# A third buffer for the weights of the first FFN layer, loads issued by two engines, and a new issue order, in a fused attention and FFN kernel

## The chip, the cores and the metric

The kernel runs on one core of one Trainium2 chip. The metric is the device time of one execution in microseconds (us), the median of several runs. One execution of each kernel was also recorded by the hardware profiler.

## The reference

One transformer block on x of 2048 rows and 576 columns, all in bf16. Attention has 32 heads of 18 and works in four segments of 512 rows: inside a segment it is causal softmax attention, and what came in earlier segments is read from a small memory M with its norm z. The FFN goes from 576 to 4608 and back. Cut to what matters:

```python
# in attention, on layernorm(x); for each segment s of 512 rows
logits = einsum('bhqd,bhkd->bhqk', qs, ks) * scale + mask
a_dot = einsum('bhqk,bhkd->bhqd', softmax(logits), vs)
pq = phi(qs)                                   # t + 1 if t > 0, else exp(t)
a_mem = einsum('bhld,bhde->bhle', pq, M) / (einsum('bhld,bhd->bhl', pq, z) + 1e-6)
o = g * a_mem + (1 - g) * a_dot                # g = sigmoid(beta)
M, z = M + phi(ks)^T @ vs, z + sum(phi(ks))
# then
h  = x + o @ wo
h2 = h + (gelu(layernorm(h) @ w1 + b1) @ w2 + b2)
```

## The kernel before

One function computes all of it, in eight chunks of 256 rows (two tiles of 128). For each chunk there are these streams of work:

- P: layernorm of a tile of x, its transpose xT, the products with wq, wk and wv (L612, and L613 for the last 65 of the contraction's rows), and their eviction from PSUM to qk_pad and v_aug (L706 to L711). The first chunk is transposed by TensorE (L657 for x, L755 for qk_pad) and moved by L692 and L693; later ones by DMA transposes, all through the helper at L367, which SP issues. xT, QT, KT, o_col and xn2T come from there.
- A: scores (L841, TensorE in a tiling of 32 rows), exp of 2048 columns at a time by ScalarE (L847), the causal mask by GpSimd or VectorE (L852, L854), and weighted values (L873, in a tiling of 32 columns). M is built at L799 and read at L910.
- B: the product with wo (also through L612), the residual, the second layernorm, and its transpose xn2T. h goes out to DRAM as hd and comes back later as hc.
- F1: the first FFN layer. F is cut into 9 groups of 512 columns. A group has four "tails" (the last 64 rows of the contraction, L1185, in a tiling of 64 rows) and 16 main matmuls (L1198); VectorE or ScalarE adds b1 on the way out of PSUM (L1208, L1206), and ScalarE applies gelu (L1220). A part of chunk 0 goes another way (L1158, L1160, with xz holding the tail rows).
- F2: the second layer (L1254), its eviction with the residual (L1258) and the output DMAs (L1265, L1267).

Short matmuls of pq with itself ("fillers", L1326) keep TensorE going while nothing else is ready at the start. They need pq, which VectorE clears (L568).

w2 stays in SBUF. w1 doesn't: each group is loaded again for each chunk, 512 KB for the mains (L1105) and two pieces of 32 KB for the tails (L1108). Two buffers, w1g0 and w1g1, take the loads in turn; the first loads also go into three pieces of the second hidden buffer hT1 while that is unused, and from load 45 on three pieces of the buffer of wq, wk and wv are used as well, since these are no longer needed.

All DMAs are issued by SP: the inputs (x at L531, weights at L534 and L535, beta at L576), w1 and w2 (L1112), the transposes, and the way out and back of h (hd, hc).

The order of the work comes from three things. A planner written into the kernel generates the operations of the streams, each with an estimated duration and with the tiles that it reads and writes. `ORDER` is a long table of operation numbers, the order in which they are issued; a negative number takes the other engine of an operation that two engines can do (`either`). `PLACE` gives the PSUM bank of each use. The engines run their queues in this order, so a waiting instruction holds up what stands behind it on its engine. What of the order concerns one engine is shown in the section on the change.

Of the kernel before, what the change touches and what calls it, by code (L numbers as in the profile page):

```python
# [16 lines left out]
def kernel(  # L17
# [41 lines left out]
    def sbuf(name, shape, dt=BF16):  # L59
# [294 lines left out]
    def transfer(o, kb, first, rd, wr, receipt=0.0):  # L354
# [3 lines left out]
        note(d, rd, wr)  # L358
        mark(d, rd, wr)
        return d  # L360

    def dma(kb, issue, rd=(), wr=(), slack=0.0):
        return transfer(op("SP", 0.5, issue, rd, wr, slack), kb, 1.6, rd, wr, {288: 0.1, 144: 0.7, 576: 0.8, 72: 0.6, 864: 1.4}.get(kb, 1.0))

    def dma_t(blocks, dst, src, rd, wr, slack=0.0):

        o = op("SP", 1.25, lambda: nc.sync.dma_start_transpose(out=dst, in_=src), rd, wr, slack)  # L367
        return transfer(o, blocks * 45 + 70, 1.4, rd, wr, 0.2)

    def begin(o, eng=None):  # L370
# [1015 lines left out]
```

## Time and profile before

| | us |
|---|---|
| median of 3 runs (lowest, highest) | 459.45 (458.41, 460.61) |
| the profiled execution | 458.34 |
| its span in the trace | 456.6 |
| TensorE busy | 448.5 |
| ScalarE busy | 315.3 |
| VectorE busy | 286.9 |
| GpSimd busy | 147.4 |
| DMA bytes moved | 83.39 MB |

The span runs from the first to the last recorded instruction; the execution's time has 1.74 us around it. In the profile's rows PE is TensorE's matmuls, PEld its loads of weights, DVE VectorE, ACT ScalarE, POOL GpSimd and SP SyncE; SPq marks the issuing of a DMA on SP's queue. A row of the timeline has its start, its duration, the engine, the line, the operation, output and inputs, the count of equal rows that it stands for, and in brackets the idle time before it with what ended that. A row of the list of waits has the waiting engine, tile and line, what it waited for, and then the total, the count and the longest wait.

### The profile page before, as it was taken

How to read it: one execution, taken by the hardware profiler on the slowest of the kernel's cores; microseconds unless marked ns; L12 is line 12 of the kernel's file. 1: busy time of each engine (PE TensorE's matmuls, PEld its weight loads, DVE VectorE, ACT ScalarE, POOL GpSimd, SP SyncE). 2: the span in 40 equal slices, each digit the busy share in tenths (PEclk: the TensorE clock that was granted, in tenths of full speed). 3: DMA queues.
4: the chain of work that ended last, by engine and by line, in shares of the span. 5: the costliest groups of instructions: out<-in, count | busy, mean ns of one | idle time of the engine just before them, and what ended most of it. 6: DMA issues, size and time to landing. Idle time of an engine off the chain costs nothing.

```text
span 456.6 us, 14417 instructions
## 1 busy us (share of the span) xinstructions
PE 448.5 (98%) x6074; PEld 333.2 (73%) x6074; DVE 286.9 (63%) x761; ACT 315.3 (69%) x316; POOL 147.4 (32%) x202
## 2 busy tenths in 40 slices
PE   7999999999999999999999999999999999999997
PEld 5776776666777777776567777667788888888874
DVE  6998888887786767876765686678672532211101
ACT  5999889976887965797786876978932354366230
POOL 4776423564373033436512333233210020000000
PEclk9999999999999999999999999999999999999999
DMA  7989998969798987787796679987778767575001
GB/s 227 329 252 264 193 184 201 182 176 178 166 251 156 232 202 178 195 177 135 204 176 165 180 194 165 201 201 156 192 193 213 196 194 191 161 208 157 27 14 39
DMA packets 137491, 83.39 MB, mean 183 GB/s; under 512 B 72786, under 2 KB 135634, under 8 KB 137426
## 3 DMA queue, kind: packets, MB, share of 16 engines
q1 hardware_dynamic: 137426, 82.47, 76.5%
q8 instruction: 47, 0.77, 0.7%
q14 instruction: 18, 0.15, 0.1%
HBM read 59.43 MB, written 6.49 MB: 144 GB/s over the span
## 4 chain that ended last, share of the span: by engine, by line
PE 89%; DMA 5%; SPq 3%; ACT 1%; DVE 1%; issue 1%; ACTq 0%
PE bank L1254 21%; PE bank L1198 17%; PE bank L612 13%; PE late L1254 6%; PE late L1198 6%; PE st L841 5%; PE ox L873 4%; PE bank L613 3%; PE bank L1185 3%; PE bank L1158 2%; PE ox L1254 1%; PE ox L1198 1%; SPq L367 1%; DMA hT<-in_B_w_dram 1%; DMA w1g<-in_B_w_dram 1%; DMA beta_row<-in_A_beta_dram 1%
## 5 line engine op out<-in xcount | busy, mean ns | idle before, releaser
L847 ACT ACTIVATE pt<-st 128x2048 bf16<-128x2048 f32 x80 | 150.1, 1877 | 41.9 <-PE st L841 21.2
L1254 PEld LDWEIGHTS <-hT 128*128 128x128 bf16 x1152 | 109.4, 98 | 29.6 <-issue 0.8
L1254 PE MATMUL bank<-w_sb,hT 128*128 128x288 bf16 x864 | 126.3, 286 | 0.0
L1198 PE MATMUL bank<-xn2T,w1g 128*128 128x256 bf16 x656 | 85.3, 273 | 0.0
L852 POOL TENSOR_SCALAR_AFFINE_SELECT pt<-pt 128x512 bf16<-128x512 bf16 x81 | 52.4, 658 | 95.2 <-ACT pt L847 88.8
L1198 PEld LDWEIGHTS <-w1g 128*128 128x128 bf16 x768 | 71.4, 98 | 16.2 <-issue 6.1
L1208 DVE TENSOR_TENSOR hT<-bank,b1T 128x512 bf16<-128x512 f32 x70 | 47.3, 685 | 41.5 <-PE bank L1198 41.1
L1220 ACT ACTIVATE hT<-hT 128x1536 bf16<-128x1536 bf16 (+3 forms) x24 | 65.7, 2768 | 0.2
L612 PE MATMUL bank<-wqkv,xT 128*128 128x432 bf16 (+1 forms) x268 | 57.1, 336 | 0.9 <-DMA xT<-xn 0.8
L612 PEld LDWEIGHTS <-xT 128*128 128x128 bf16 x400 | 36.9, 97 | 19.8 <-DMA xT<-xn 0.9
L1206 ACT ACTIVATE hT<-late,b1T 128x256 bf16<-128x256 f32 x32 | 13.3, 477 | 38.7 <-PE late L1198 22.3
L1258 DVE TENSOR_TENSOR ot<-bank,hc 128x288 bf16<-128x288 f32 x24 | 11.0, 456 | 43.0 <-PE bank L1254 38.0
L1206 ACT ACTIVATE hT<-bank,b1T 128x256 bf16<-128x256 f32 x56 | 23.5, 473 | 20.1 <-PE bank L1198 20.1
L1254 PE MATMUL late<-w_sb,hT 128*128 128x288 bf16 (+1 forms) x216 | 33.9, 296 | 0.0
L841 PE MATMUL st<-QT,KT 32*128 32x128 bf16 x1280 | 32.4, 217 | 0.5 <-issue 0.5
L841 PEld LDWEIGHTS <-KT 32*128 32x128 bf16 x1280 | 18.7, 92 | 15.2 <-issue 11.9
L1198 PEld LDWEIGHTS <-wqkv 128*128 128x128 bf16 x272 | 26.0, 98 | 4.6 <-issue 0.8
L854 DVE TENSOR_TENSOR pt<-pt,causal 128x512 bf16<-128x512 bf16 x47 | 22.4, 479 | 8.3 <-ACT pt L847 8.1
L646 POOL TENSOR_TENSOR rstd_b<-rstd_b,mhalf 128x1 f32<-128x1 f32 x16 | 9.3, 582 | 56.2 <-DVE rstd_b L636 53.8
L873 PE MATMUL ox<-pt,v_aug 128*32 128x128 bf16 x1184 | 26.3, 221 | 0.0
L873 PEld LDWEIGHTS <-v_aug 128*32 128x32 bf16 x1184 | 17.2, 96 | 10.6 <-issue 8.2
L613 PE MATMUL bank<-wqkv,xT 65*128 65x432 bf16 (+1 forms) x67 | 22.6, 338 | 0.0
(156 smaller groups left out, 642.0 us busy)
## 6 DMA issues: line engine op xcount, KB each, us to landing
w1g<-in_B_w_dram SPq DMA_DIRECT2D x50, 512.0 KB, 4.1
wqkv<-in_B_w_dram SPq DMA_DIRECT2D x17, 512.0 KB, 3.9
w_sb<-in_B_w_dram SPq DMA_DIRECT2D x6, 864.0 KB, 7.7
hd<-h_t SPq DMA_DIRECT2D x14, 288.0 KB, 4.2
hc<-hd SPq DMA_DIRECT2D x28, 144.0 KB, 2.9
w1g<-in_B_w_dram SPq DMA_DIRECT2D x100, 32.0 KB, 3.2
x_b<-in_A_x_dram SPq DMA_DIRECT2D x18, 144.0 KB, 3.0
hT<-in_B_w_dram SPq DMA_DIRECT2D x5, 512.0 KB, 6.0
```

Of the source, the lines that this page charges most:

```text
L612: nc.tensor.matmul(out=out_ap, lhsT=lhsT_of(slice(0, P), k), rhs=rhs_of(slice(0, P), k), start=(k == 0), stop=False)
L613: nc.tensor.matmul(out=out_ap, lhsT=lhsT_of(slice(0, KTAIL), 4), rhs=rhs_of(slice(0, KTAIL), 4), start=False, stop=True)
L841: nc.tensor.matmul(out=st4[:, i, n * P:(n + 1) * P], lhsT=KTs[(c - c % 2 + kt // 2) % 3][rows, g, (kt % 2) * P:(kt % 2 + 1) * P], rhs=QTs[ ...
L847: op("ACT", 1.88, lambda: nc.scalar.activation(out=pt[:], in_=st4[:], func=ACT.Exp, scale=scale), sk, [("pt", slot, n) for n in range(4)], ...
L852: either(("POOL", 0.64, lambda part=part: nc.gpsimd.affine_select(out=part, in_=part, pattern=[[0, 4], [1, P]], compare_op=ALU.is_ge, fill ...
L854: ("DVE", 0.42, lambda part=part: nc.vector.tensor_tensor(out=part, in0=part, in1=causal[:].unsqueeze(1).to_broadcast([P, 4, P]), op=ALU.m ...
L873: nc.tensor.matmul(out=ox[32 * i:32 * i + 32, g % 4 * P:(g % 4 + 1) * P], lhsT=v_flat[(2 * s0 + kt) % 6][:, h * E:h * E + 32], rhs=pts[slo ...
L1198: nc.tensor.matmul(out=bank(b)[:, a * Q:(a + 1) * Q], lhsT=w1_main(wt)[:, k, (2 * (h % 2) + a) * P:(2 * (h % 2) + a + 1) * P], rhs=xn2T[c ...
L1206: nc.scalar.activation(out=hT[:, f + a, :], in_=bank(b)[:, a * Q:(a + 1) * Q], func=ACT.Identity, bias=b1T[:, f + a:f + a + 1])
L1208: either(("DVE", 0.69, lambda hT=hT, f=f, b=b: nc.vector.tensor_tensor(out=hT[:, f:f + 2, :], in0=bank(b)[:].rearrange("p (a w) -> p a w", ...
L1220: op("ACT", (f1 - f0) * Q * 0.00083 + 0.18, lambda hT=hT, f0=f0, f1=f1: nc.scalar.activation(out=hT[:, f0:f1, :], in_=hT[:, f0:f1, :], fun ...
L1254: nc.tensor.matmul(out=acc, lhsT=hT[:, q, tl * P:(tl + 1) * P], rhs=w2_sb[:, q, hs], start=(q == 0), stop=(q == NF - 1))
```

## The change

- w1 gets three buffers (w1g0 to w1g2). The loads ahead of use become groups 0 to 5, later ones follow a period of three, and of six from load 45 on. A group's matmuls may be planned only once its load has been.
- Room for that: xn2T has three buffers instead of four, so that the transpose of chunk c waits for the first layer of chunk c - 3. beta_row, ones and b1_rows move into the bytes of t1, and xz into those of t2, both of which are written from later chunks on.
- `dma_two` lets a DMA be issued by SP or by ScalarE. It is used for the first four loads of x, the weights of attention, beta, b1, b2, and all of w1.
- The first two tiles of x come in two halves of 64 rows each, and wq, wk and wv in two halves of 288 columns, each with a key of its own, so that a product needs only its half.
- After attention the five PSUM banks of scores and weighted values become banks 3 to 7 of `PLACE`.
- `ORDER` and `PLACE` were searched anew, with longer issues of SP in the planner's picture of it.

All lines move down: L1105 becomes L1121, L1108 L1124, L612 L628, L657 L673, L755 L771, L847 L863, L1254 L1271, L1326 L1343, L367 L373.

The core of the diff (the table's lines left out):

```diff
+    def dma_two(kb, issue, rd=(), wr=(), slack=0.0):
+        o = either(("SP", 0.5, lambda: issue(nc.sync)), ("ACT", 0.55, lambda: issue(nc.scalar)), rd, wr, slack)
+        return transfer(o, kb, 1.6, rd, wr, {288: 0.1, 144: 0.7, 576: 0.8, 72: 0.6, 864: 1.4}.get(kb, 1.0))
...
-    w1_bufs = [sbuf(f"w1g{j}", [W1]) for j in range(2)]
+    w1_bufs = [sbuf(f"w1g{j}", [W1]) for j in range(3)]
...
+    NX = 3
-    xn2T = [sbuf(f"xn2T{j}", [KT, Q]) for j in range(4)]
+    xn2T = [sbuf(f"xn2T{j}", [KT, Q]) for j in range(NX)]
...
+    early = t1[:].rearrange("p h e -> p (h e)").bitcast(BF16)
+    ones, beta_row, b1_rows = early[:, 0:P], early[:, P:P + H], early[:, 2 * P:3 * P]
+    xz = t2[:].rearrange("p h e -> p (h e)").bitcast(BF16)[:, 0:2 * Q].rearrange("p (h q) -> p h q", h=2)
...
     for tl in range(2):
-        load_x(tl, x_p[tl], ("x_p", tl))
+        for h in range(2):
+            dma_two(72, lambda e, tl=tl, h=h: e.dma_start(out=x_p[tl][64 * h:64 * h + 64, :], in_=x[tl * P + 64 * h:tl * P + 64 * h + 64, :]),
+                    (), [("x_p", tl, h)])
     for j, W in enumerate((A_wq, A_wk, A_wv)):
-        weights(wqkv, slice(j * D, (j + 1) * D), W, f"wqkv{j}")
+        for h in range(2):
+            to = slice(j * D + h * HALF, j * D + (h + 1) * HALF)
+            dma_two(290, lambda e, to=to, h=h, W=W: e.dma_start(
+                out=wqkv[:, 0:4, to], in_=W[0:512, h * HALF:(h + 1) * HALF].rearrange("(k p) n -> p k n", p=P)), (), [f"wqkv{j}{h}"])
...
-                yield need(lambda: c < 4 or c - 4 in done_F1, idle=False)
-                dma_t(KT, xn2T_part, xn2[tl][:], [("xn2", tl)], [("xn2T", c % 4, tl)], SLACK["t_h"])
+                yield need(lambda: c < NX or c - NX in done_F1, idle=False)
+                dma_t(KT, xn2T_part, xn2[tl][:], [("xn2", tl)], [("xn2T", c % NX, tl)], SLACK["t_h"])
...
-        dma(512, lambda: nc.sync.dma_start(out=w1_main(wt), in_=B_w1[0:512, fcols].rearrange("(k p) f -> p k f", p=P)), (), [k], SLACK["w1"])
+        dma_two(512, lambda e: e.dma_start(out=w1_main(wt), in_=B_w1[0:512, fcols].rearrange("(k p) f -> p k f", p=P)), (), [k], SLACK["w1"])
```

What the new tables do to an engine's queue is seen in its rows (line, operation, output and inputs, shape). VectorE at the very start, before: the memsets of padding come ahead of that of pq, on which the fillers wait.

```order
L539 MEMSET ones 1x128
L539 MEMSET xn_1_86 128x32
L539 MEMSET qk_pad_96 128x64x7
L539 MEMSET v_aug_101 128x32
L568 MEMSET pq 128x256
L539 MEMSET maskcol 128x1
```

And in the changed kernel:

```order
L583 MEMSET pq 128x256
L548 MEMSET maskcol 128x1
L548 MEMSET v_aug_96 128x32
L548 MEMSET v_aug_98 128x32
L548 MEMSET v_aug_99 128x32
L548 MEMSET qk_pad_92 128x64x7
```

The memset of pq has moved to the front. On TensorE, 22 fillers now stand ahead of the first transposes instead of 13, and 4 instead of 10 behind them; then the product of the first tile with the first half of wq comes ahead of the second tile's transposes, which stood ahead of all products before.

SP around the first transpose of chunk 4's xn2T (that is xn2T_92 here), before: w1g_67 and w1g_68 are the two buffers of w1, 128x4x512 a group's mains and 64x256 one of its two tails.

```order
L367 DMA_TRANSPOSE KT_108<-qk_pad_97 128x8x128
L1105 DMA w1g_68<-in_B_w_dram 128x4x512
L367 DMA_TRANSPOSE xn2T_92<-xn_0_87 128x5x128
L1108 DMA w1g_68<-in_B_w_dram 64x256
L367 DMA_TRANSPOSE xT_91<-o_nat_114 128x5x128
L367 DMA_TRANSPOSE KT_108<-qk_pad_96 128x8x128
L1105 DMA w1g_67<-in_B_w_dram 128x4x512
L1108 DMA w1g_67<-in_B_w_dram 64x256 x2
```

The same place in the changed kernel, where that tile is xn2T_90 and the buffers are w1g_65 to w1g_67:

```order
L373 DMA_TRANSPOSE xT_87<-o_nat_110 128x5x128
L1256 DMA hc<-hd 128x288
L1124 DMA w1g_67<-in_B_w_dram 64x256
L1074 DMA hd<-h_t_120 128x576
L373 DMA_TRANSPOSE xn2T_90<-xn_0_84 128x5x128
L1124 DMA w1g_66<-in_B_w_dram 64x256 x2
L1121 DMA w1g_66<-in_B_w_dram 128x4x512
L1124 DMA w1g_67<-in_B_w_dram 64x256 x2
L1121 DMA w1g_67<-in_B_w_dram 128x4x512
```

Three transposes stood between the loads of two groups, and now the loads of two groups follow on one transpose.

ScalarE between the first gelu (L1220) and the next evictions of FFN values, before: exps (L847, of the scores st into pt) with the small work of the other streams.

```order
L1220 ACTIVATE hT_128<-hT_128 128x3584
L847 ACT_TABLE_LOAD
L847 ACTIVATE pt_111<-st_155 128x2048
L710 CAST qk_pad_97<-bank_149 128x24x18
L710 CAST v_aug_101<-bank_150 128x8x18
L847 ACTIVATE pt_112<-st_155 128x2048
```

The same place in the changed kernel:

```order
L1237 ACTIVATE hT_124<-hT_124 128x3584
L863 ACT_TABLE_LOAD
L863 ACTIVATE pt_107<-st_151 128x2048
L726 CAST qk_pad_92<-bank_147 128x16x18
L1121 DMA w1g_67<-in_B_w_dram 128x4x512
L726 CAST v_aug_96<-bank_147 128x8x18
L1124 DMA w1g_66<-in_B_w_dram 64x256
L863 ACTIVATE pt_108<-st_151 128x2048
L912 ACTIVATE ek<-QT_102 128x512
L1124 DMA w1g_67<-in_B_w_dram 64x256
L863 ACTIVATE pt_107<-st_151 128x2048
```

Loads of w1 now stand between the exps, in ScalarE's own queue. At the other end of the program, the last product on TensorE before was 20 matmuls of 144 columns behind 20 of 432; now the 144 columns come earlier, and the last are 24 matmuls of 432 columns.

More of the change, by code (lines that the diff above doesn't have):

```diff
@@ L453, in bank @@
         return banks["bank", place[k.serial]] if isinstance(k, Bank) else banks[k]
-    beta_row = sbuf("beta_row", [H])
-    ones = sbuf("ones", [P])
     wqkv = sbuf("wqkv", [KT, 3 * D])
@@ L512, with dynamic_swap @@
     late = []
-    def swap():
+    def dynamic_swap():
         st_pool.__exit__(None, None, None)
@@ L517, in swap @@
         for i in range(4):
-            banks["st", i] = pool.tile([P, 512], F32, name=f"late{i}")
+            banks["bank", 3 + i] = pool.tile([P, 512], F32, name=f"late{i}")
+        banks["bank", 7] = ox
     bank_slots.free.append("ox")
@@ L575, in constants @@
         memset("DVE", 0.06, mhalf[:], -0.5, "mhalf")
-        dma(9, lambda: nc.sync.dma_start(out=beta_row[0:1, :], in_=A_beta.rearrange("(o h) -> o h", o=1)), (), ["beta"])
+        dma_two(9, lambda e: e.dma_start(out=beta_row[0:1, :], in_=A_beta.rearrange("(o h) -> o h", o=1)), (), ["beta"])
         memset("POOL", 0.12, causal[:], BIG, "causal")
@@ L582, in constants @@
         for tl in range(2):
-            layernorm(f"p{tl}", x_p[tl][:], ("x_p", tl), xn1[tl], ("xn1", tl), False, SLACK["ln0"] + 3 * tl, late_scale=True)
+            layernorm(f"p{tl}", x_p[tl][:], ("x_p", tl), xn1[tl], ("xn1", tl), False, SLACK["ln0"] + 3 * tl, late_scale=True,
+                      also=[("x_p", tl, h) for h in range(2)])
         for j in range(2, 6):
@@ L621, in half @@
         def half(c):
-            op("DVE", 0.455, lambda: nc.vector.bn_stats(out=stats[:, c, :], in_=src[:, c * HALF:(c + 1) * HALF]), [skey], ["st" + who],
+            op("DVE", 0.455, lambda: nc.vector.bn_stats(out=stats[:, c, :], in_=src[:, c * HALF:(c + 1) * HALF]), [skey, *also], ["st" + who],
                slack=slack)
@@ L650, in layernorm @@
            slack=slack + SLACK["pow"], port=False)
-        op("DVE", 0.8 if f32 else 0.43, apply, ["st" + who, skey] + ([] if late_scale else ["rs" + who]), [dkey], slack=slack + fast,
+        op("DVE", 0.8 if f32 else 0.43, apply, ["st" + who, skey, *also] + ([] if late_scale else ["rs" + who]), [dkey], slack=slack + fast,
            port=True).two = f32
@@ L1002, in stream_A @@
                             done_A.add(c)
-        bank_slots.free.append("ox")
-        st = [("st", i) for i in range(4)]
-        op("POOL", 0.0, swap, (), st, slack=-1000, port=False)
-        bank_slots.free += st
+        more = [("bank", 3 + i) for i in range(5)]
+        op("POOL", 0.0, dynamic_swap, (), [("st", i) for i in range(4)] + ["ox"] + more, slack=-1000, port=False)
+        bank_slots.free += more
         late.append(True)
@@ L1134, in stream_F1 @@
         for c in range(NCH):
[L1135 removed]
+            xk = [("xn2T", c % NX, 0), ("xn2T", c % NX, 1)]
             hT = hTs[c % 2]
@@ L1176, in stream_F1 @@
                 wk = [key for _, k in w1s for key in (k, (*k, 0), (*k, 1))]
-                yield need(lambda: c in done_B and (c < 2 or c - 2 in done_F2), bank_slots, xk + wk, mode=64, n=2 * len(some))
+                yield need(lambda: c in done_B and (c < 2 or c - 2 in done_F2) and some[-1] < w1_next[0], bank_slots, xk + wk, mode=64,
+                           n=2 * len(some))
                 bs = [bank_slots.take() for _ in range(2 * len(some))]
```

62 lines of the change are left out of this document (32 added, 30 removed), and 231 rows, old and new, of the table ORDER.

## The prediction

> **What bounds the kernel now.** I read the page's busy times first, then TensorE's list of waits, then the timeline at both ends and the chain of waits behind the two longest stops.
>
> ```profile
> span 456.6 us, 14417 instructions
> PE 448.5 (98%) x6074; PEld 333.2 (73%) x6074; DVE 286.9 (63%) x761; ACT 315.3 (69%) x316; POOL 147.4 (32%) x202
> ```
>
> TensorE (PE) is busy for 448.5 of 456.6 us, so the end is set by TensorE's own work plus 8.1 us in which it stands still. The profiled execution took 458.34 us, 1.74 us around its span, and lies 1.11 us below the median of 459.45 us. I make the sum against 458.34 and move the result up by 1.11 at the end. TensorE's waits, each with its total, its count and its longest:
>
> ```profile
> PE ox L1326 <- DVE maskcol L539: 2.0, 1, 2.0
> PE bank L1185 <- DMA w1g<-in_B_w_dram: 0.9, 1, 0.9
> PE bank L612 <- DMA xT<-xn: 0.8, 1, 0.8
> PE st L841 <- issue: 0.5, 1, 0.5
> PE bank L1198 <- DMA hT<-in_B_w_dram: 0.4, 1, 0.4
> PE bank L612 <- DMA xT<-o_nat: 0.3, 1, 0.3
> PE bank L550 <- DMA beta_row<-in_A_beta_dram: 0.2, 1, 0.2
> PE bank L1160 <- issue: 0.2, 1, 0.2
> ```
>
> Of the 8.1 us, 2.0 stand ahead of the first matmul, 3.3 are the seven stops below that row, and the other 2.8 lie in the end behind the last matmul. Transfers are late for only 2.4 us (0.9 + 0.8 + 0.4 + 0.3) after the start. That is the most that loads which come earlier can give there. The change leaves TensorE's products as they are (6079 matmuls instead of 6074, and the five are fillers), so a gain has to come out of the 8.1 us.
>
> **The two long stops** have the same history. The chain of waits around 211 and 234 us, and the mean landing time of a group's load from the page:
>
> ```profile
> 211.93 4.12 DMA xT<-xn
> 233.33 1.21 SPq L367
> 234.59 4.79 DMA w1g<-in_B_w_dram
> w1g<-in_B_w_dram SPq DMA_DIRECT2D x50, 512.0 KB, 4.1
> ```
>
> SP issues everything, and each DMA transpose (L367) holds its queue for over 1.2 us. The w1g tail that TensorE wanted at 239.43 was issued at 234.59 behind such rows, and then took 4.79 us. With two buffers a group's load can start only when the group two before it has been read; with three it is asked for one group earlier. I added up TensorE's durations from the trace between the last read of a buffer's old content and the first read of its new one, in both issued orders: the median is 12.2 us before and 16.9 after, and mains with less than 8 us fall from 17 of 67 to 2 of 66. Against 4.1 us to land, the two stops on w1 (0.9 and 0.4, the latter in the spare buffers) should go nearly to nothing; I leave 0.1. The xT stops (0.8 + 0.3) hang on transposes, and these stay on SP. SP has 348 issues instead of 416, so its pile-ups are shorter; I leave 0.7 of 1.1. **Waits: 2.4 becomes 0.8, so -1.6 us**; bounds -2.4 (none is left) and +1.0 (a new stop as long as the longest of these rows).
>
> **The start.** Rows of the timeline (start, duration):
>
> ```profile
> 1.68 0.27 DVE L568 MEMSET pq<- 128x256 uint32 x1
> 2.01 0.82 PE L1326 MATMUL ox<-pq 128*128 128x256 bf16 x3 [2.01 <-DVE maskcol L539]
> 3.05 1.91 PE L1326 MATMUL bank<-pq 128*128 128x256 bf16 x8
> 4.75 0.74 PE L657 MATMUL ox<-ident,xn 128*128 128x128 bf16 x5
> 5.29 1.50 PE L1326 MATMUL bank<-pq 128*128 128x256 bf16 x10
> 7.10 0.45 PE L657 MATMUL bank<-ident,xn 128*128 128x128 bf16 x5
> 7.50 0.65 PE L612 MATMUL bank<-wqkv,xT 128*128 128x288 bf16 x4
> 7.59 0.49 DVE L693 COPY xT<-bank 128x640 bf16<-128x640 bf16 x1 [1.54 <-PE bank L657]
> 9.00 0.50 ACT L706 ACTIVATE qk_pad<-bank,rstd_p 128x288 bf16<-128x288 f32 x1 [1.60 <-PE bank L613]
> ```
>
> The fillers (L1326) need pq. VectorE clears it at 1.68 behind other memsets; in the new order it does this first, so TensorE can start near 0.88 + 0.27, about 1.2. Eight fillers start from 3.05 to 4.75, 0.2125 us each; the ten from 5.29 take 1.50 in all, so the last ones run at about half of that (0.11, an estimate), from some 3.8 us after TensorE's first row. The new order has 22 fillers ahead of the first transposes: 18 of 0.2125 bring TensorE to 5.0, 4 of 0.11 to 5.45. Then come five transposes (0.45), the copy of xT (0.49, under four more fillers), and the first product at about 6.35 instead of 7.50: 1.15 earlier, without the wait for beta. About 0.5 is given back: the eight transposes of qk_pad (L755) now come right behind the second half of wq's product and five transposes of 0.45, and both halves have to be evicted before (0.50 each, the row at 9.00). **Start: -0.65**; bounds -1.15 and +0.3 (both evictions uncovered, and wq's second half late).
>
> Whether the weights are there is seen in the windows of one us (columns: five engines, granted clock, busy share of the DMA engines, GB/s):
>
> ```profile
> 3.00:4.00 1.00, 1.00 (x7) 0.70 (x5) 0.87 (x3) 1.00 (x4) 0.00 (x0) 1.00 0.72 152
> 4.00:5.00 1.00, 1.00 (x8) 0.70 (x7) 0.96 (x4) 0.52 (x2) 0.00 (x0) 1.00 0.95 311
> ```
>
> Ahead of the first product must land: x (288 KB), two tails of 72 KB and one half of wq (288 KB), 720 KB, that is 2.3 us at 311 GB/s from about 2 us on. So the halves, not the second issuer, free this path. The share of 0.72 in 3 to 4 us is the only gap in which a quicker issue could put bytes. Here a rule speaks against part of the change. The Trainium skill, page "DMA: Bandwidth & Descriptors", section "Issuing engines are not separate DMA queues", says that DMAs begun by several engines run on the same 16 DMA engines, and that only the issuing time is saved. The row of 0.72 agrees that no more than 0.28 us of DMA time is open there; by the rule alone the start would gain about 0.3 and the time would be 458.8 us.
>
> **Array modes.** Counted over both programs, TensorE goes from one tiling of the array to another 288 times instead of 280. A piece of 12 matmuls that ends in such a change, and one of 8 that ends without:
>
> ```profile
> 301.29 1.64 PE L1254 MATMUL bank<-w_sb,hT 128*128 128x288 bf16 x12
> 302.86 0.41 PE L873 MATMUL ox<-pt,v_aug 128*32 128x128 bf16 x16
> ...
> 105.95 1.14 PE L1254 MATMUL bank<-w_sb,hT 128*128 128x288 bf16 x8
> ...
> 106.93 0.30 PE L910 MATMUL bank<-MZ_blk,pq 128*128 128x76 bf16 x4
> ```
>
> From start to start 8 take 0.98, 0.1225 each; 12 would take 1.47 and take 1.57, so a change is 0.10 us. **Eight more: +0.8**; bounds +0.4 and +0.9.
>
> **The end.**
>
> ```profile
> 452.83 0.61 DVE L1258 TENSOR_TENSOR ot<-late,h_t 128x432 bf16<-128x432 f32 x1 [3.32 <-PE late L1254]
> 453.47 1.13 SPq L1265 DMA_DIRECT2D out_dram<-ot  x2
> 453.93 0.31 DVE L1258 TENSOR_TENSOR ot<-ox,h_t 128x144 bf16<-128x144 f32 x1 [0.49 <-PE ox L1254]
> ```
>
> The last product is now 144 columns wide (eviction 0.31); in the new order it is 432 wide (0.61), +0.30. Of the two output DMAs of the second row, issued at 453.47 and 454.27, the wide one landed after 1.67 us and the narrow one after 1.49, +0.18. **End: +0.5**; bounds 0 (if the wide DMA is split over free engines just as fast) and +0.6.
>
> **What ScalarE (ACT) issues.** The new program gives it 73 DMAs: seven at the start, 33 between the exps, and the rest where only the second layer's work is left. It also loads activation tables 14 times instead of 12. The window from 40 to 130 us, the exps, and SP's issues of loads:
>
> ```profile
> 40.00:130.00 90.00, 88.98 (x1486) 63.43 (x1484) 75.27 (x199) 74.76 (x71) 42.24 (x54) 1.00 0.92 191
> L847 ACT ACTIVATE pt<-st 128x2048 bf16<-128x2048 f32 x80 | 150.1, 1877 | 41.9 <-PE st L841 21.2
> ...
> 234.59 0.59 SPq L1108 DMA_DIRECT2D w1g<-in_B_w_dram  x1
> ...
> 17.73 2.24 SPq L1105 DMA_DIRECT2D hT<-in_B_w_dram  x1
> ```
>
> No row shows an issue by ScalarE. Its nearest are SP's for the same loads: 0.59 without a crowd, 2.24 in one. I take 0.59, since the load that I compare with is the same and ScalarE issues them singly between exps. In the part of the program that answers to 40 to 130 us stand 13 of them: 13 x 0.59 = 7.7 us, inside ScalarE's idle 90.0 - 74.76 = 15.2. So the cover is that idle time: **0 us on TensorE**. If the cover is gone, all of it is paid. A wait that ScalarE now takes on itself is new: a main that has to wait until TensorE has read the buffer holds up the next exp behind it, and TensorE's weighted values (L873) wait for that exp. SP shows how long such waits can be:
>
> ```profile
> SPq L1105 <- PE late L1198: 13.8, 8, 3.9
> SPq L1105 <- PE bank L1198: 6.3, 5, 3.9
> ```
>
> Bounds: 0 (below nothing is excluded, as a busier ScalarE speeds nothing up) and 13 x 2.24 - 15.2 = +13.9.
>
> **At no cost**: xn2T with three buffers (a transpose then waits for the first layer of three chunks before, work that lies some tens of us back; its cost, if that fails, is one transpose's 1.21 us on SP). beta, ones, b1 and xz lie in t1 and t2, which are written only in later chunks. The swap of PSUM banks falls after attention. The x halves add two issues at the start.
>
> **Sum**: -1.6 - 0.65 + 0.8 + 0.5 + 0 = -0.95; 458.34 becomes 457.4, and on the median **458.5 us**. Its own range is 456.8 to 460.5 us.
>
> **The rivals.**
> - A, all transfers are on time: waits -2.4, start -1.15, the two "issue" stops of 0.7 moved away by the new order, modes +0.8, end +0.5: -2.95, **456.5 us**. For it speaks the median lead of 16.9 us; against it, that the xT stops lie on transposes.
> - B, slower: ScalarE's issues hold up the exps between 40 and 130 us. The point from which it decides is 15.2 / 13 = 1.17 us for each. At 1.5 us (13 x 1.5 = 19.5, 4.3 over the cover) the sum is -0.95 + 4.3 = +3.35, **462.8 us**. For it: 2.24 in a crowd, and SP's waits of up to 3.9 on the buffers. Against it: 0.59, and a third buffer that is free earlier.
> - C, the change does not do what it says: the stops come from SP's transposes, and a third buffer leaves them. The waits of 2.4 stay, so start -0.65, modes +0.8 and end +0.5 are left, +0.65: **460.1 us**. For it: both long stops have an L367 row in their chain; against it, the leads.
> - D, the rule on issuers above, as a mechanism here: the start gains 0.3 and the rest is as forecast, **458.8 us**.
>
> **Chances.** About 0.5% (2.3 us) is what a measurement of this kernel can tell from no change: 457.15 to 461.75. The forecast has 0.30, C 0.12, D 0.08: within the bound 0.50. A and times below it 0.31; B 0.19. The range leaves out about 0.2: below 455.3 (A with no price for modes and end either, -2.95 - 1.3 = -4.25, 455.2) 0.08, above 463.0 (B beyond 1.5 us each) 0.10.
>
> **What would show it.** Right: the first filler near 1.2 and the first product near 6.35 us; no stop of TensorE on w1g or hT over 0.3 us; ScalarE's issues near 0.6; the last eviction 0.61. Wrong: a list of TensorE's waits with pt or st behind ScalarE at the head (B), xT still at 1.1 (C), or a TensorE that is busy for longer than 449.3, which would mean that the new order slows matmuls in a way that I have not priced.

## The result and the profile after

| | before | changed |
|---|---|---|
| median of 20 runs each, us | 459.54 | 463.02 |
| lowest to highest, us | 458.29 to 462.62 | 459.75 to 467.34 |
| the profiled execution, us | 458.34 | 464.59 |
| its span, us | 456.6 | 462.9 |

The changed kernel is slower: 1.0057 times the time before, 95% interval 1.0036 to 1.0078. The ratio leaves one disturbed execution of the changed kernel out (467.34 us, with a granted clock of 0.992); that of the two medians is 1.0076. So the loss is 2.6 us by the ratio and 3.5 by the medians. The profiled execution lies 1.6 us above the median of its kernel, and that of before 1.2 us below its own; the 6.3 us between the two spans are therefore about twice what the kernels differ by, and are read for where they come from and not for how much.

The page of the changed kernel, the same two lines:

```profile
span 462.9 us, 14450 instructions
PE 450.7 (97%) x6079; PEld 333.9 (72%) x6079; DVE 286.1 (62%) x768; ACT 315.0 (68%) x310; POOL 146.1 (32%) x199
```

TensorE works 2.2 us longer and stands still for 12.2 us instead of 8.1. Of the 2.2 us, 0.8 are the fillers, which start earlier (their rows cover 5.6 us instead of 4.7). Its list of waits, all that the view has:

```profile
PE bank L628 <- DMA xT<-o_nat: 1.8, 2, 0.9
PE bank L1174 <- DVE hT L1180: 1.7, 1, 1.7
PE bank L1271 <- ACT hT L1223: 1.4, 1, 1.4
PE bank L1343 <- DVE pq L583: 1.2, 1, 1.2
PE bank L815 <- issue: 1.1, 1, 1.1
PE bank L1202 <- ACT hT L1223: 0.7, 1, 0.7
PE bank L628 <- DMA wqkv<-in_A_wq_dram: 0.3, 1, 0.3
```

The stops on w1g, hT and xT<-xn are no longer there. In their place stand a longer one on xT<-o_nat, and three behind VectorE and ScalarE, which evict FFN values too late (L1180, L1223). VectorE's own wait for the transposed output of attention, before and after:

```profile
DVE r L932 <- DMA o_col<-oT: 1.0, 3, 0.4
```

```profile
DVE r L949 <- DMA o_col<-oT: 9.0, 6, 4.4
```

Where the time was lost is seen in how far TensorE lags at equal work. For this the matmuls of a profile are given the mean time of their shape over all traces compared, fillers none, and added up in the order of the program; the table has the time at which the changed kernel, and two of the experiments below, had done as much as before at the time on the left.

| time before, us | changed | mains on SP | two tails on SP |
|---|---|---|---|
| 30 | +0.2 | +0.3 | +0.4 |
| 48 | -0.2 | -0.1 | 0.0 |
| 68 | +3.4 | +1.6 | +0.4 |
| 100 | +2.8 | +2.3 | -0.3 |
| 134 | +5.4 | +3.3 | +1.7 |
| 250 | +3.1 | +1.6 | -0.6 |
| 265 | +5.2 | +1.6 | -0.6 |
| 453 | +5.5 | +1.8 | -0.4 |

The changed kernel loses 3.6 us between 48 and 68 us, 2.6 between 100 and 134, wins 2.3 between 134 and 250 where before had its two long stops, and loses 2.1 just behind.

The last column is also a check on these readings. Up to 254 us the kernel with two tails on SP (e13 below) issues exactly what the changed kernel issues, and yet its trace is 3.0 us less behind at 68 us and 3.7 at 250. That of e14 below, which differs only at the end, lies between (about 2.0, 3.5 and 1.2 us behind at 68, 134 and 250). So traces of one order differ by microseconds from execution to execution, and a loss belongs to the order only where it recurs. The 3.6 us up to 68 do not (0.4 in e13, 1.5 in e14). Between 100 and 134 both lose 2.0, against 1.0 with the mains on SP, and both win the 2.3 us between 134 and 250.

The chain of waits at the three places of loss:

```profile
57.01 5.70 DMA o_col<-oT
62.73 0.25 DVE r L949
62.99 0.56 DVE hT L1180
```

```profile
110.99 4.76 DMA xT<-o_nat
...
122.58 4.57 DMA xT<-o_nat
```

```profile
251.95 7.14 DMA out_dram<-ot
...
259.16 0.47 ACTq L1124
```

At the first two places the chains hang on DMA transposes that took 4.6 to 5.7 us from issue to landing. (The one of o_col, 5.70 here, took 4.24 in e13 and 3.05 in e14.) What ScalarE did beside the second pair, from its timeline (ACTq is the issue of a DMA in ScalarE's queue):

```profile
110.44 0.37 ACTq L1121 DMA_DIRECT2D w1g<-in_B_w_dram  x1
121.07 0.37 ACTq L1121 DMA_DIRECT2D w1g<-in_B_w_dram  x1
```

In each case a main of w1, 512 KB, was issued by ScalarE within 1.5 us ahead of the transpose (another at 56.71, ahead of o_col). The third place is different. ScalarE's timeline there:

```profile
254.94 0.47 ACTq L1124 DMA_DIRECT2D w1g<-in_B_w_dram  x1
255.52 0.84 ACT L1223 ACTIVATE hT<-bank,b1T 128x256 bf16<-128x256 f32 x2 [2.26 <-DVE MZ_blk L836]
259.16 0.47 ACTq L1124 DMA_DIRECT2D w1g<-in_B_w_dram  x1
259.73 0.55 ACTq L1121 DMA_DIRECT2D w1g<-in_B_w_dram  x1
260.38 1.88 ACT L863 ACTIVATE pt<-st 128x2048 bf16<-128x2048 f32 x1 [4.02 <-issue]
262.15 0.83 ACT L1223 ACTIVATE hT<-bank,b1T 128x256 bf16<-128x256 f32 x2
```

From 256.4 to 259.16 its queue stands at the issue of a 32 KB tail, and the chain names what it waited for: an output DMA that SP had issued at 251.95 and that landed after 7.14 us. (Every DMA of this program, of either engine, takes one of eight completion semaphores in turn; the trace has 421 DMAs, 52 or 53 on each. The issue waits until the DMA before it on that semaphore has landed: of 310 such pairs with a recorded landing, none has the issue first.) Behind the tail wait an exp and the eviction that TensorE needs at 263. The issues themselves are cheap, 0.37 to 0.55 us.

### The profile page after: what moved, and what is told of

Same layout as the page of the kernel before. It is cut to its first block, busy times and chain, and to the rows that moved or that the text cites. A ratio compares the mean times of both kernels' runs of the same rounds, so it can differ in the third digit from the quotient of the medians.

```text
span 462.9 us, 14450 instructions
## 1 busy us (share of the span) xinstructions
PE 450.7 (97%) x6079; PEld 333.9 (72%) x6079; DVE 286.1 (62%) x768; ACT 315.0 (68%) x310; POOL 146.1 (32%) x199
## 4 chain that ended last, share of the span: by engine, by line
PE 90%; DMA 6%; ACT 1%; issue 1%; ACTq 0%; DVE 0%; SPq 0%; POOL 0%; DVEq 0%; POOLq 0%
PE bank L1271 23%; PE bank L1215 17%; PE bank L628 13%; PE late L1215 6%; PE st L857 5%; PE late L1271 5%; PE ox L889 5%; PE bank L629 3%; PE bank L1202 3%; DMA xT<-o_nat 2%; PE ox L1271 2%; DMA out_dram<-ot 2%; PE bank L1174 1%; DMA o_col<-oT 1%; ACT pt L863 1%; DMA wqkv<-in_A_wq_dram 1%
## 5 line engine op out<-in xcount | busy, mean ns | idle before, releaser
L863 ACT ACTIVATE pt<-st 128x2048 bf16<-128x2048 f32 x80 | 150.2, 1878 | 48.0 <-PE st L857 23.4
L1271 PEld LDWEIGHTS <-hT 128*128 128x128 bf16 x1152 | 109.0, 98 | 31.8 <-issue 3.1
L1271 PE MATMUL bank<-w_sb,hT 128*128 128x288 bf16 (+1 forms) x900 | 126.9, 284 | 1.4 <-ACT hT L1223 1.4
L1215 PEld LDWEIGHTS <-w1g 128*128 128x128 bf16 x816 | 75.9, 98 | 17.1 <-issue 6.7
L1215 PE MATMUL bank<-xn2T,w1g 128*128 128x256 bf16 x672 | 86.9, 273 | 0.0
L1225 DVE TENSOR_TENSOR hT<-bank,b1T 128x512 bf16<-128x512 f32 x68 | 46.1, 687 | 27.2 <-PE bank L1215 25.5
L628 PE MATMUL bank<-wqkv,xT 128*128 128x432 bf16 (+1 forms) x264 | 56.4, 336 | 0.3 <-DMA wqkv<-in_A_wq_dram 0.3
L628 PEld LDWEIGHTS <-xT 128*128 128x128 bf16 x400 | 36.9, 97 | 21.6 <-DMA xT<-o_nat 2.2
L1223 ACT ACTIVATE hT<-bank,b1T 128x256 bf16<-128x256 f32 x54 | 22.6, 474 | 22.2 <-PE bank L1215 18.3
L1223 ACT ACTIVATE hT<-late,b1T 128x256 bf16<-128x256 f32 x30 | 12.5, 473 | 29.7 <-PE late L1215 26.8
L1271 PE MATMUL late<-w_sb,hT 128*128 128x288 bf16 (+1 forms) x180 | 28.5, 298 | 0.0
L1225 DVE TENSOR_TENSOR hT<-late,b1T 128x512 bf16<-128x512 f32 x19 | 12.9, 688 | 25.2 <-PE late L1215 25.1
L889 PE MATMUL ox<-pt,v_aug 128*32 128x128 bf16 x1184 | 27.6, 221 | 0.1
L1073 POOL TENSOR_TENSOR h_t<-h_t,b_bc 128x576 f32<-128x576 f32 x16 | 20.8, 1298 | 18.3 <-DVE xn L646 9.2
L1215 PEld LDWEIGHTS <-wqkv 128*128 128x128 bf16 x240 | 23.2, 98 | 3.7 <-issue 0.4
```

The lines of the kernel that those rows point to most:

```text
L628: nc.tensor.matmul(out=out_ap, lhsT=lhsT_of(slice(0, P), k), rhs=rhs_of(slice(0, P), k), start=(k == 0), stop=False)
L863: op("ACT", 1.88, lambda: nc.scalar.activation(out=pt[:], in_=st4[:], func=ACT.Exp, scale=scale), sk, [("pt", slot, n) for n in range(4)], ...
L889: nc.tensor.matmul(out=ox[32 * i:32 * i + 32, g % 4 * P:(g % 4 + 1) * P], lhsT=v_flat[(2 * s0 + kt) % 6][:, h * E:h * E + 32], rhs=pts[slo ...
L1073: op("POOL", 1.29, lambda: nc.gpsimd.tensor_tensor(out=h_t[:], in0=h_t[:], in1=b2_bc[:], op=ALU.add), ["b2"], [("h", tl)], slack=SLACK["hb"])
L1215: nc.tensor.matmul(out=bank(b)[:, a * Q:(a + 1) * Q], lhsT=w1_main(wt)[:, k, (2 * (h % 2) + a) * P:(2 * (h % 2) + a + 1) * P], rhs=xn2T[c ...
L1223: nc.scalar.activation(out=hT[:, f + a, :], in_=bank(b)[:, a * Q:(a + 1) * Q], func=ACT.Identity, bias=b1T[:, f + a:f + a + 1])
```

## The experiments

Three theories came out of this. **Q**: a big load from ScalarE runs beside SP's transposes instead of in line with them, and these land late. **H**: ScalarE's queue is held by a load whose turn has not come, with exps and evictions behind it. Rival **O**: it is the new issue order, whoever issues. Each kernel was timed against the kernel before on the same chip, in 6 to 12 executions (the change in 20); the chip is not the same for all rows, so ratios are compared and not medians.

| run | ratio to before | interval | median, us |
|---|---|---|---|
| the change | 1.0057 | 1.0036 to 1.0078 | 463.02 |
| e1, all of w1 on SP | 1.0093 | 1.0062 to 1.0125 | 463.61 |
| e2, every DMA on SP | 1.0102 | 1.0066 to 1.0139 | 464.09 |
| e3, mains on SP | 1.0017 | 0.9996 to 1.0038 | 461.01 |
| e4, tails on SP | 1.0129 | 1.0084 to 1.0174 | 466.55 |
| e5, e3 and seven finishes later | 1.0042 | 1.0016 to 1.0068 | 460.97 |
| e6, before with a third of the mains on ScalarE | 1.0125 | 1.0087 to 1.0163 | 465.15 |
| e7, before with a third of the tails on ScalarE | 1.0022 | 1.0000 to 1.0044 | 460.10 |
| e8, three mains on SP | 1.0066 | 1.0040 to 1.0093 | 461.49 |
| e9, three mains and two tails on SP | 1.0010 | 0.9987 to 1.0034 | 460.15 |
| e10, mains and two tails on SP, narrow product last | 0.9996 | 0.9976 to 1.0015 | 459.07 |
| e11, before with two SP issues moved | 0.9970 | 0.9951 to 0.9989 | 458.35 |
| e12, the same, one of them less far | 0.9972 | 0.9951 to 0.9992 | 458.90 |
| e13, two tails on SP | 1.0033 | 1.0013 to 1.0052 | 461.27 |
| e14, narrow product last | 1.0063 | 1.0038 to 1.0087 | 463.08 |

### Who issues w1: e1 to e4

A load is marked with its size, and its choice of ScalarE is overruled:

```diff
         o = either(("SP", 0.5, lambda: issue(nc.sync)), ("ACT", 0.55, lambda: issue(nc.scalar)), rd, wr, slack)
+        o.load = kb
...
-                o.eng, (o.dur, o.issue) = list((o.ways or o.spare).items())[i < 0]
+                o.eng, (o.dur, o.issue) = list((o.ways or o.spare).items())[i < 0 and not (getattr(o, "load", 0) in (45, 512))]
```

That is e1. e2 overrules every load (`getattr(o, "load", 0)`), e3 only `== 512`, e4 only `== 45`.

> The changed kernel, with every load of w1 issued by SP again, at the same place of the order; ScalarE keeps only its five issues at the start and the one for the tail of wo. Theory Q (ScalarE's issues cost the time: its queue stands still until an earlier DMA of SP has landed, and its loads run beside SP's transposes and make these land late): the stops near 63, 116, 127, 256 and 263 us of the changed kernel, 7 us in all, mostly go, so 458 to 460 us, as before the change or a little under. Rival O (the new order itself is slower, whoever issues): it stays at 462 to 463. Rival S (SP's queue is what cannot take more issues): above 464.

> The changed kernel with every DMA issued by SP, the first ones too. Against the run with only w1 on SP it tells what ScalarE's issues at the start are worth. If two issuers help the start, 0.5 to 1.5 us slower than that run, since seven more issues of about 0.6 us stand in SP's queue ahead of the first product; if they only run beside SP's on the same DMA engines, no difference (within 0.5 us).

> The changed kernel with the mains of w1 (512 KB) on SP and the tails (32 KB) still on ScalarE. If the loss comes from big loads that run beside SP's transposes, nearly all of it comes back: 459 to 460 us. If it comes from ScalarE's queue standing still behind earlier DMAs, which tails do as well as mains, most of it stays: 461.5 to 463. Rival O: 462 to 463, with the stops at other places than behind ScalarE.

> The mirror image: tails on SP, mains on ScalarE. Big loads beside transposes: 461.5 to 463, as slow as the changed kernel. ScalarE's queue standing still: about half comes back, 460 to 461.5, since the tails are half of its issues among the exps. Rival O: 462 to 463.

e1 fell between the theories: 1.0093. With everything back on SP the order is no faster, if anything slower, so Q and H in their simple form fell: part of the loss is in the order, which counts on ScalarE for some issues (rival S of the expectation, in part). e2 gave 1.0102, not to be told from e1, so what two issuers bring at the start stays open. e3 and e4 split the change in two: with the mains on SP and the tails on ScalarE the loss shrinks to 1.0017, and the other way round it grows to 1.0129. So tails from ScalarE help this order (the intervals lie apart in both pairs, e3 and e1, the change and e4), and mains from ScalarE hurt it (here the intervals of e3 and the change just touch, and those of e1 and e4 overlap). In e3 the same transpose of xT that took 4.76 us in the changed kernel is issued at 110.1 with the main behind it on SP. The view of that tile has

```profile
L374 SPq DMA_TRANSPOSE xT<-o_nat x1: 1209/1209/1209, 110.1 to 110.1; - x1
...
DMA to landing us min/median/max: 2.8/2.8/2.8
```

and TensorE's stops on xT<-o_nat are gone from e3's list. The eleven traces of the new order agree on this transpose: it takes 4.6 to 5.1 us in the four kernels in which ScalarE issues that main, from 0.9 us ahead of it to 0.5 behind (the change, e4, e13, e14), and 2.8 to 3.0 in the seven in which SP issues it, 2.6 to 3.6 us behind (e1, e2, e3, e5, e8, e9, e10). VectorE's wait for o_col is another matter. It is as long where SP issues every main, in e1 and in e3, so it comes with the new order and not with ScalarE's loads (it is 3.2 us in e14's trace and 6.9 to 11.2 in the others of this order but e5's). Its rows in e1 and e3:

```profile
DVE r L950 <- DMA o_col<-oT: 11.2, 7, 2.0
```

```profile
DVE r L950 <- DMA o_col<-oT: 8.1, 7, 2.2
```

### The mechanism in the old order: e6 and e7

The kernel before, with one line changed: the mains of every third group (e6), or its tails (e7), are issued by ScalarE.

```diff
-        dma(512, lambda: nc.sync.dma_start(out=w1_main(wt), ...
+        dma(512, lambda: (nc.scalar if n % 3 == 0 and n >= 9 else nc.sync).dma_start(out=w1_main(wt), ...
```

> The kernel before, in its own order and with two buffers, with the mains of every third group of w1 (21 of 67 loads, 512 KB) issued by ScalarE instead of SP. Theory Q (big loads from ScalarE run beside SP's transposes and make these land late, and hold ScalarE's queue): 1.5 to 4 us slower than before, with new stops of TensorE on xT or behind VectorE's wait for o_col. Rival O (it lies in the searched order alone): within 1 us of before.

> The kernel before with the two tails of every third group (42 loads of 32 KB) issued by ScalarE. If small loads from ScalarE cost little and free SP, within 1 us of before or up to 1 us faster; if what costs is that ScalarE's queue stands still, 1 to 3 us slower.

e6 is the clearest of all runs: 21 loads on another engine, nothing else, cost 1.25%, more than the whole change. e7 costs 0.22%, with an interval from nothing to 0.44. In e6 TensorE waits

```profile
PE bank L612 <- DMA xT<-xn: 2.7, 2, 1.9
...
PE bank L612 <- DMA xT<-o_nat: 1.8, 1, 1.8
PE bank L1185 <- DMA w1g<-in_B_w_dram: 1.6, 2, 1.4
PE bank L1198 <- DMA hT<-in_B_w_dram: 0.8, 1, 0.8
```

One transpose of xT shows it side by side, the same row of SP's queue. Before, with a main that SP issued behind it at 124.86:

```profile
L367 SPq DMA_TRANSPOSE xT<-o_nat x1: 1212/1212/1212, 122.9 to 122.9; - x1
...
DMA to landing us min/median/max: 2.9/2.9/2.9
```

In e6, with that main issued by ScalarE at 123.81:

```profile
L367 SPq DMA_TRANSPOSE xT<-o_nat x1: 1205/1205/1205, 123.5 to 123.5; - x1
...
  PE bank L612: 1.8, 1
DMA to landing us min/median/max: 5.6/5.6/5.6
```

```profile
123.73 1.88 ACT L847 ACTIVATE pt<-st 128x2048 bf16<-128x2048 f32 x1 [0.27 <-PE st L841]
123.81 0.38 ACTq L1105 DMA_DIRECT2D w1g<-in_B_w_dram  x1
```

The transpose was issued 0.34 us ahead of the main and still took 5.6 us instead of 2.9, while ScalarE itself went on with its exp. So here ScalarE's time plays no part. The Trainium skill, page "DMA: Bandwidth & Descriptors", section "Issuing engines are not separate DMA queues", says that DMAs begun by different engines run on the same 16 DMA engines and interleave; the 2.9 and 5.6 us agree with that.

What makes a transpose late is then a big load near it, and not the engine that issued the load. Counted over all traces but that of e2, a transpose takes 3.21 us in the median with no main issued from 2.5 us ahead of it to 1 us behind (547 transposes), 4.61 with one that SP issued (278), and 4.56 with one that ScalarE issued (54). Of the transposes whose landing is recorded, 25 of 57 had a main so near before the change, and 24 of 63 have one in the changed kernel. The number is much the same; the difference lies in which transposes they are, and whether TensorE waits for them.

### VectorE's wait for o_col: e5

A finish is the three instructions in which VectorE divides the attention's output by its sum. This is e3 with the finishes held back until two FFN evictions of VectorE have gone by, for the seven ahead of which VectorE stood still:

```diff
+    def later_finishes(order):
+        late = [o for k in (1, 2, 3, 14, 20, 24, 26) for o in finishes[k]]
+        held, seen = [], 0
+        for o in order:
+            if o in late:
+                seen = seen if held else 0
+                held.append(o)
+                continue
...
-        for o in arranged():
+        for o in later_finishes(arranged()):
```

> The run with mains on SP and tails on ScalarE, and seven of the 28 steps in which VectorE divides the attention's output (r from o_col, three instructions) put two FFN evictions later in the order: those seven ahead of which VectorE stood still. Theory V (what is left of the loss is VectorE, which waits for o_col's transposes with FFN evictions behind it that TensorE waits for): VectorE's wait for o_col falls from 8 us to under 3, TensorE's stops near 70 us (1.4 us) go, 458.5 to 459.8 us, 1 to 2.5 us under the run with mains on SP. Rival (the stops only move to the products with wo, which wait for the same division later): within 0.5 us of 461.

The wait fell from 8.1 to 0.2 us, but the time did not follow: the ratio is 1.0042 against 1.0017, and the intervals overlap. TensorE's stops of 1.0 and 0.2 us behind hT became several of 0.3 to 0.5 behind h_t, hT, xT and pq (that behind pt is in e3 too):

```profile
PE bank L817 <- DVE h_t L1054: 0.5, 1, 0.5
PE bank L1206 <- DVE hT L1184: 0.5, 1, 0.5
PE st L859 <- ACT pt L865: 0.5, 1, 0.5
...
PE bank L928 <- DVE pq L921: 0.4, 1, 0.4
```

The rival held: what follows from the division is late as well, and taking VectorE out of the way of the late o_col gives nothing back.

### ScalarE's held queue: e8, e9, e13

In e8 the second, fifth and sixth main that ScalarE issues go to SP; in e9 these and two tails, and in e13 the two tails alone (`loads` counts ScalarE's w1 loads).

```diff
+                mine = i < 0 and getattr(o, "load", 0) in (45, 512)
+                loads += mine
-                o.eng, (o.dur, o.issue) = list((o.ways or o.spare).items())[i < 0]
+                o.eng, (o.dur, o.issue) = list((o.ways or o.spare).items())[i < 0 and not (mine and (loads in (2, 11, 12, 29, 30)))]
```

> The changed kernel with only three of ScalarE's mains given back to SP, those that were issued at 56.7, 110.4 and 121.1 us, each within a microsecond or two ahead of a transpose (o_col, xT, xT) that then landed after 4.6 to 5.7 us. Theory Q: the stops of 1.9, 1.1 and 1.0 us at 63.6, 115.8 and 127.2 us go and the rest stays, 2.5 to 4 us under the changed kernel, 459 to 460.5 us; the stops near 256 and 263 us (2.4 us) are still there. Rival (SP's queue, now longer by three, lets other things be late): less than 1 us.

> The changed kernel with the same three mains on SP as in the run with three, and also the two tails that ScalarE issued at 254.9 and 259.2 us of the changed kernel. The second of these stood still until an output DMA of SP had landed, 7.1 us after its issue, with an exp and the FFN evictions behind it on ScalarE. Theory H (ScalarE's queue held by a load): TensorE's stops near 253 and 260 us (2.6 us in the run with three mains) go, about 459.5 us. Rival R (it is the main that ScalarE issued at 250.7 us, beside o_col's and KT's transposes, that makes all of SP's DMAs land late): these stops stay over 1.5 us, 461 to 462 us.

> The changed kernel with only the two tails of 254.9 and 259.2 us on SP, all else as in the change. Theory H (ScalarE's queue held by a load that waits for an earlier DMA): the stops near 256 and 263 us, 2.4 us, go, and the ratio to before falls from 1.0057 to about 1.001 to 1.003. Theory Q alone (only the mains beside the transposes count): no change, 1.005 to 1.007.

In e8's trace the stop at 63.6 is gone, that at 116 too, and that at 127 is down to 0.4; those behind ScalarE remain:

```profile
PE bank L1272 <- ACT hT L1224: 1.8, 1, 1.8
PE ox L629 <- DVE xT L710: 1.5, 1, 1.5
...
PE bank L1203 <- ACT hT L1224: 0.7, 1, 0.7
PE bank L629 <- DMA xT<-o_nat: 0.4, 1, 0.4
```

The stops on xT behaved as Q says. That at 63.6 tells nothing, since it is absent from e13 and e14 too, where its main stays on ScalarE. And the time did not follow: 1.0066 against 1.0057, no gain that this measurement resolves, where 2.5 to 4 us were expected (the three stops come to 3.5 us in TensorE's list). With two tails of 32 KB moved as well, e9 comes to 1.0010, and no stop behind ScalarE's evictions is left in its list. e13, the two tails alone, comes to 1.0033; the first of the three rows of its list is

```profile
PE bank L629 <- DMA xT<-o_nat: 1.3, 2, 0.8
...
```

(The trace of e13 was taken in an execution 2.6 us below the median of its kernel, so it shows less than the usual loss.) H is shown at this place: an issue of 0.5 us held ScalarE for 2.8 us, and without the two tails both stops are gone, in e9 and in e13. In time they are worth 1 us (e13 against the change, intervals that overlap) to 2.5 us (e9 against e8, intervals that do not). But a hold has no fixed price, and the tails are not the only loads that make one. In e3 the second tail stays on ScalarE and holds it from 253.3 to 256.16 us, and no stop follows: there the main of 259.73 does not stand between it and the exp. In e4 the tails are on SP, and the next main is held in their place until an earlier main has landed; a stop of 1.4 us behind an eviction of ScalarE stays. e4's chain:

```profile
249.80 8.24 DMA w1g<-in_B_w_dram
...
258.12 0.37 ACTq L1122
```

The two stops on xT stay in e13 and go in e9, which is what Q says.

### The end: e14 and e10

The last five steps of the 144-column product, with its eviction and its output DMA, are put at the end of the order again; e10 has that together with all mains and the two tails on SP.

```diff
+    def narrow_last(order):
+        held = narrows[-5:]
+        for o in order:
+            if o.made > narrows[-1].made and any(p in held for p in o.inner):
+                held.append(o)
+        rest = [o for o in order if o not in held]
+        held.sort(key=order.index)
+        rest += held
+        return rest
```

> The run with all mains on SP and the tails on ScalarE, without those two tails on ScalarE, and with the last product's 144 columns at the very end again, as before the change. From the rows of both profiles the end shrinks by 0.8 us (from 3.8 to 3.0 us between the last matmul's start and the end of the span), and the stop near 259 us goes: 459.5 to 460.3 us, about 1 us under the run with mains on SP (461.0). If the end counts only as overlap, no change from 461.0.

> The changed kernel with the last product's 144 columns at the very end again and nothing else. From the rows of both profiles the end should shrink by 0.5 us (the forecast's own term) to 0.8 us (what the two spans differ by behind the last matmul's start), so a ratio 0.001 to 0.002 below the changed kernel's 1.0057, and the last two rows of the profile as before the change.

The last eviction is 0.31 us again in e14, where it was 0.61 in the changed kernel:

```profile
459.52 0.61 DVE L1275 TENSOR_TENSOR ot<-late,h_t 128x432 bf16<-128x432 f32 x1 [1.71 <-PE late L1271]
```

```profile
456.51 0.31 DVE L1279 TENSOR_TENSOR ot<-bank,h_t 128x144 bf16<-128x144 f32 x1 [0.49 <-PE bank L1273]
```

From the start of the last matmul to the end of the span it is 2.9 us before, 3.8 in the changed kernel and 3.1 in e14. The profile gives 0.7 us back; in the times this is not seen (1.0063), as 0.7 us is less than half the width of the interval. e10 is at 0.9996, level with before: the change without its big loads on ScalarE, without two held issues and with the old end costs nothing and brings nothing.

### SP's order in the old kernel: e11 and e12

The two long stops of before can also be met by moving two issues of SP. `sp` is the list of SP's instructions; the transpose of xT goes ahead of an output DMA and a tail, and the late tail of w1 ahead of QT's transpose. In e12 the first pair is (208, 207), so that xT passes only the tail.

```diff
+        order = list(arranged())
+        sp = [o for o in order if o.eng == "SP"]
+        for late, early in ((208, 206), (227, 223)):
+            o, at = sp[late], order.index(sp[early])
+            order.remove(o)
+            order.insert(at, o)
```

> The kernel before, with two of SP's issues moved: the transpose of xT at 211.9 us goes ahead of an output DMA and a tail of w1, and the tail of w1 at 234.6 us goes ahead of two transposes, a main and another transpose. Nothing else is changed. If SP's order alone makes the two long stops of before (0.8 and 0.9 us), they go and nothing takes their place: 457.3 to 458.5 us, under both kernels. If these stops only hide others (the next thing that is late), within 0.5 us of before.

> The kernel before with the tail of w1 moved as in the run with two moves, and the transpose of xT moved ahead of the tail of w1 only, so that the output DMA stays where it was. In the profile of the run with two moves VectorE waited for that output DMA and TensorE for VectorE, 1.3 us at 217.6 us. If that new stop is the price of the second move: 0.5 to 1.3 us under the run with two moves (458.35), 457.1 to 457.9 us. If not, the same within 0.5 us.

Both are faster than before (0.9970 and 0.9972, intervals below 1) and so than the changed kernel, with no third buffer. The stop on w1g at 239 us is gone in both. In e11 that on xT turned into one behind VectorE, which waits for the output DMA that now comes later; in e12 it is 0.6 instead of 0.8:

```profile
PE bank L612 <- DVE ot L1258: 1.3, 1, 1.3
```

```profile
PE bank L612 <- DMA xT<-xn: 0.6, 1, 0.6
```

The new stop's price was expected to come back in e12 and did not; the two cannot be told apart in time. So the stop on w1g that the third buffer was to remove goes with one moved issue, too.

## Why the prediction was wrong

The forecast was 458.5 us and faster; measured were 463.02 us, slower. By its steps:

- **The step that failed is the term 0 for what ScalarE issues.** It bounded the price of an issue (0.59 taken, 2.24 the upper end) and set 13 of them against ScalarE's idle 15.2 us. The 13 issues cost 0.37 to 0.50 each, less than was taken, and their sum lies well inside ScalarE's idle time. The cost came from two things that a price per issue does not hold: mains that no longer stand in SP's line run beside transposes that TensorE waits for (shown by e6 in the old order, 1.25%, and in the new one by e3, where 1.0057 becomes 1.0017 and the same transpose takes 2.8 us instead of 4.8), and an issue that waits for an earlier DMA holds the exps and evictions behind it (2.8 us at 256 us; shown by e9 and e13). The text did name a wait that ScalarE takes on itself, but only for a buffer that TensorE is still reading, not for the landing of another DMA. An estimate from the ratios: of the 3.6 us between the forecast's -0.95 and the measured +2.6, 1.8 go when the mains leave ScalarE (e3) and 2.2 when three mains and two tails do (e9), each uncertain by more than 1 us; the rest lies in the terms below and in the order itself.
- **Rival B** had the right sign, and exps that are held are a part of what happened; that its 462.8 us lie so near is luck. Its point of decision, 1.17 us for each issue between 40 and 130 us, was never reached, and the holds that cost time lie at 253 to 260 us.
- **Waits, -1.6**: half right. The stops on w1g and hT, 1.3 us, went, as the longer lead of the loads had promised, and that on xT<-xn too; in the table of lags the changed kernel wins 2.3 us there. But the 0.7 us left for xT became 1.8 on xT<-o_nat, and the o_col transposes, behind which VectorE now stands for 9.0 us instead of 1.0, were not in the sum at all. The sum took the landing times of transposes as they were before; they depend on what else is under way.
- **The start, -0.65**: about 0 (the lag is +0.2 us at 30 us). The first filler came at 1.24 (1.2 forecast), the first transposes at 5.55 (5.45) and the first product at 6.58 (6.35). Then the second half of wq was late, which the bounds named but the value left out:

```profile
6.03 0.49 DVE L709 COPY xT<-bank 128x640 bf16<-128x640 bf16 x1 [0.49 <-PE bank L673]
...
6.58 0.66 PE L628 MATMUL ox<-wqkv,xT 128*128 128x288 bf16 x4
...
8.24 0.65 PE L628 MATMUL bank<-wqkv,xT 128*128 128x288 bf16 x4 [0.32 <-DMA wqkv<-in_A_wq_dram]
```

- **Array modes, +0.8**: right. Added up over each trace, what a matmul ahead of a change of tiling takes over the mean of its shape, from its start to the next one's, is 31.7 us in 280 changes before and 32.6 in 288 after, 0.11 each: +0.9.
- **The end, +0.5**: right in kind, 0.9 in the profile (2.9 to 3.8 us) and so above its upper bound of 0.6, since the wider last matmul itself was not counted, nor the whole of the output DMA.
- **TensorE's busy time** of 450.7 us is over the 449.3 that were named as a sign of matmuls that run slower. Of the 1.4 us over, 0.8 are the fillers, which the sum had moved out of the idle time at the start without adding them to the busy time.
- **C and D**: the stops that the third buffer was for are gone, against C. Whether the buffer or the new order did it is not shown, as no run has the one without the other. Of the other issuer's effect at the start nothing could be told from e2, so D stays open.

Open remain the "issue" stops of 1.1 us (50 us), which are there in the change, in e3 and in some of the others and not in e4, and e1's loss of 0.93%. With the tails on ScalarE (e3) 0.17% of it is left, but which late issue of SP costs the rest was not traced.

## What to carry to other kernels

A big load makes a small urgent transfer beside it late, whichever engine issued the load. In the queue of the engine that issues both, the load's place behind the transfer keeps it apart in time, here by 1.9 to 3.6 us, while the transfer took 2.8 to 3.0; issued by another engine, it came anywhere from 1.5 us ahead to 0.5 behind, and the transfer took 4.6 to 5.6. So before big loads go to a second issuer, look at which transfers they will meet there, and keep them in line with those that something waits for; small loads can be moved with less harm (e7), or to advantage (e3 against e1). On an engine that computes, ask of each issue not what it costs but what it may wait for, and what stands behind it. And before a loss in one trace is put down to a cause, look for it in the trace of another kernel that issues the same up to there.

## What the runs showed of the hardware that was not expected

A transpose that was issued 0.34 us ahead of a 512 KB load of another engine still took 5.6 us instead of 2.9; being first in time did not help it. And two executions that issue the same up to 254 us stood 3.7 us apart at 250 us (the change and e13), at a granted clock of 1.000 in both.
